# Attention over a cached K and V: the small load of x moves from the sync queue's second place to the head of ScalarE's queue

## The chip, the cores and the metric

The kernel runs on one core of a Trainium2 chip. The time is that of one execution on the device in microseconds. The kernel before takes 184.4 us, the median of three runs (184.36 to 184.57).

## The reference

A block of grouped-query attention for 8 sequences with 4 new tokens each. All arrays are bf16.

```
B, Sq, D = 8, 4, 512 ;  Hq, Hkv, Sk, Dh = 32, 8, 2048, 128 ;  rep = Hq // Hkv = 4
q = (x @ wq)                     # x [8,4,512], wq [512,4096] -> 32 heads of 128
s = q @ k_cache^T * Dh**-0.5     # k_cache [8,8,2048,128], each head of K serves 4 of q
p = softmax(s) ;  o = p @ v_cache
out = o @ wo                     # wo [4096,512] -> [8,4,512]
```

K and V are 33.6 MB each, wq and wo 4.2 MB each, x and the output 32 KB each. So nearly all of the 75.5 MB that are read are used once.

## The kernel before

**Staging.** K and V go through a ring of four slots in SBUF (`ring`, `NR = 4`), each of 4 MB, that is 32 KB in each of the 128 partitions. wq and wo pass through the same ring, a slot each. The list `loads` gives their order: K0 and x together ("k0"), wq, K1, V0, K2, V1, K3, and so on to V7, then wo. `issue(done)` (line 157) issues loads while fewer than four slots are taken. The call `issue(0)` at the start thus issues K0, x, wq, K1 and V0 at once; after each step of the main loop `issue(2 + 2 * u)` asks for what has come free, and each of those issues waits on its queue until the slot's last reader is done.

**Queues.** All loads are issued on the sync engine's queue, in order, but one: K0 comes in two halves (`by_member`), the first on the sync queue and the second on ScalarE's (`load_kv`, line 133, with the engines `(nc.sync, nc.scalar)`). x follows on the sync queue (line 163) and wq behind it (line 137). A queue hands out its transfers in order; the packets of both queues are carried by the same 16 DMA engines.

**Steps.** There are eight steps of K and V (`NU = 8`); each holds 16 heads of 2048 keys divided among partitions. For each step: VectorE turns K into 32x32 blocks (`turn`, line 213), TensorE forms the scores against a block-diagonal arrangement of the queries (`scores`, line 251), VectorE takes the maxima (`top`), ScalarE the exponentials (`exps`, line 291), VectorE turns the weights (line 305), ScalarE and GpSimd put them in block-diagonal form (line 315), TensorE multiplies them with V (`values`, line 331), and short operations scale and rearrange the result. The program order is written by hand (`manual_schedule`); the values of a step come after the scores of the next.

**The beginning,** where x is used: VectorE and GpSimd clear tiles; VectorE turns the first two quarters of K0 in four operations (line 413, the first and third read the first half of K0, the second and fourth the other one). TensorE transposes x against an identity (line 416), ScalarE copies the result to SBUF as `xT_sb` (line 419), TensorE multiplies with wq in 32 matmuls (line 425), ScalarE copies the queries out (line 432), VectorE transposes them (line 436), and GpSimd spreads them in the block-diagonal tile (`queries`, line 231). Then the scores of step 0 begin.

**The end:** wo's second half is loaded in four pieces (line 146), and `project` (line 403) multiplies by each as it lands. Two copies bring the result out of PSUM (lines 482 and 483), and one DMA stores it (line 484).

Of the kernel before, what the change touches and what calls it, by code (L numbers as in the profile page):

```python
# [17 lines left out]
def kernel(  # L18
# [9 lines left out]
    nc = tc.nc  # L28
# [45 lines left out]
    x_sb = const.tile([T, D], BF16, name="x_sb")  # L74
# [13 lines left out]
    def single(u):  # L88
        return FIRST < u < LAST

    def half_of(u):
        return NG - 1 if u == LAST else 0
# [8 lines left out]
    def take(key):  # L101
        slot_of[key] = n_loads[0] % NR
        n_loads[0] += 1
        return slot_of[key]
# [5 lines left out]
    def load_kv(kind, u, parts, engines=(nc.sync,)):  # L110

        slot = take((kind, u))
        cache = k_cache if kind == "k" else v_cache
        n = C * Dh
        if not single(u):
            rows = cache[NS1:, G * half_of(u) : G * half_of(u) + G].rearrange(
                "b g (s c) d -> (g s) b (c d)", c=C
            )
        elif kind == "v":
            rows = cache[u - 1].rearrange("(b g) (s c) d -> (g s) b (c d)", g=G, c=C)  # L120
        else:
            rows = cache[u - 1].rearrange("h (s c) d -> (h s) (c d)", c=NS * C)
        if kind == "k" and single(u):
            pairs = [(ring[:, slot, :, :].rearrange("p b n -> p (b n)"), rows)]
        elif parts is by_member:
            pairs = [(ring[:, slot, b, :], rows[:, b]) for b in range(NB)]
        else:
            pairs = [
                (ring[:, slot, :, int(h0 * n) : int(h1 * n)], rows[:, :, int(h0 * n) : int(h1 * n)])
                for h0, h1 in parts  # L130
            ]
        for i, (to, of) in enumerate(pairs):
            engines[i % len(engines)].dma_start(to, of)

    def load_wq():
        slot = take("wq")
        nc.sync.dma_start(
            ring[:, slot, :, :].rearrange("p b n -> p (b n)"), wq.rearrange("(p r) n -> p (r n)", r=R)
        )

    def load_wo():
        slot = take("wo")
        for gg, cuts in ((0, (0, RW)), (1, (0, 8, 13, 15, RW))):
            rows = wo[gg * G * 512 : (gg + 1) * G * 512, :].rearrange("(p r) j -> p (r j)", r=RW)
            for r0, r1 in zip(cuts, cuts[1:]):
                nc.sync.dma_start(ring[:, slot, gg, r0 * D : r1 * D], rows[:, r0 * D : r1 * D])
# [10 lines left out]
    def issue(done):  # L157

        while loads and n_loads[0] < done + NR:
            what = loads.pop()  # L160
            if what == "k0":
                load_kv("k", 0, by_member, (nc.sync, nc.scalar))
                nc.sync.dma_start(x_sb[:, :], x.flatten_outer_dims())
            elif what == "wq":
                load_wq()
            elif what == "wo":
                load_wo()
            elif what in split:
                load_kv(*what, by_member)
            else:  # L170
                load_kv(*what, by_half if what == ("v", NU - 1) else whole)

    issue(0)

    make_identity(nc, ident[:])
# [266 lines left out]
    for u in range(NU + 1):  # L442
# [19 lines left out]
        if u >= 1:  # L462
# [7 lines left out]
            if u == NU:  # L470
                joined(u - 1)
        issue(2 + 2 * u)

    o_last = psum_o.tile([128, DH], FP32, tag="o", name="o_last")
# [40 lines left out]
```

## Time and profile before

| what | value |
|---|---|
| median of three runs | 184.4 us (184.36 to 184.57) |
| time of the profiled execution | 184.38 us |
| its span, from the first to the last instruction | 182.5 us |
| TensorE / VectorE / ScalarE / GpSimd busy | 75% / 71% / 39% / 22% of the span |
| read from HBM | 75.53 MB, 414 GB/s over the span |
| x from issue to landing | 12.1 us |
| second half of K0 (ScalarE's queue) from issue to landing | 12.4 us |
| wq from issue to landing | 21.0 us |
| the store of the output, 32 KB, from issue to landing | 1.5 us |

The span is what the profile covers; 1.9 us of the execution lie outside it. The landing times hold all the waiting that a transfer does behind others, on its own queue and on the engines that both queues share, so they tell how much is queued ahead and not what a transfer costs. q1 in the profile is the sync queue, q10 is ScalarE's; q8 and q14 carry instructions. In the profile an engine's name with a q behind it (SPq, ACTq) is its sequencer, which issues DMAs, and ACT, DVE, POOL, PE and SP are ScalarE, VectorE, GpSimd, TensorE and the sync engine.

### The profile page before, as it was taken

How to read it: one execution, taken by the hardware profiler on the slowest of the kernel's cores; microseconds unless marked ns; L12 is line 12 of the kernel's file. 1: busy time of each engine (PE TensorE's matmuls, PEld its weight loads, DVE VectorE, ACT ScalarE, POOL GpSimd, SP SyncE). 2: the span in 40 equal slices, each digit the busy share in tenths (PEclk: the TensorE clock that was granted, in tenths of full speed). 3: DMA queues.
4: the chain of work that ended last, by engine and by line, in shares of the span. 5: the costliest groups of instructions: out<-in, count | busy, mean ns of one | idle time of the engine just before them, and what ended most of it. 6: DMA issues, size and time to landing. Idle time of an engine off the chain costs nothing.

```text
span 182.5 us, 2386 instructions
## 1 busy us (share of the span) xinstructions
PE 136.6 (75%) x924; PEld 83.3 (46%) x924; DVE 128.7 (71%) x161; ACT 70.3 (39%) x91; POOL 39.3 (22%) x110
## 2 busy tenths in 40 slices
PE   0000076940999999998999898989399977899993
PEld 0000022310348635843783485358234852388971
DVE  6518025738994999599689957995399559967340
ACT  2000020019604940990395079109900792063010
POOL 8800006006200700430080035004400220023000
PEclk9999999995589999999999999999969999999999
DMA  6999999999999998999999999999999999999991
GB/s 226 431 485 395 424 460 406 424 445 449 452 384 427 456 461 382 420 460 452 391 417 453 460 402 418 431 478 424 391 435 424 435 427 435 415 426 438 427 385 42
DMA packets 4938, 75.70 MB, mean 415 GB/s; under 512 B 512, under 2 KB 704, under 8 KB 960
## 3 DMA queue, kind: packets, MB, share of 16 engines
q1 hardware_dynamic: 4784, 73.47, 94.3%
q10 hardware_dynamic: 144, 2.10, 2.8%
q8 instruction: 7, 0.11, 0.2%
q14 instruction: 3, 0.02, 0.0%
HBM read 75.53 MB, written 0.03 MB: 414 GB/s over the span
## 4 chain that ended last, share of the span: by engine, by line
DMA 42%; DVE 23%; PE 22%; issue 4%; ACT 3%; POOL 2%; SPq 1%; ACTq 0%; DVEq 0%; POOLq 0%
DMA ring<-in_wo_dram 16%; PE s_ps L251 16%; DMA ring<-in_k_cache_dram 15%; DVE kt L213 14%; DMA ring<-in_wq_dram 12%; DVE stat L264 4%; PE o_ps L331 4%; ACT p_sb L291 3%; PE psq L425 2%; DVE pt L305 2%; DVE stat L322 1%; POOL p_bd L315 1%; POOL q_bd L231 1%; PE s_ps L403 1%; DVE stat L272 0%
## 5 line engine op out<-in xcount | busy, mean ns | idle before, releaser
L251 PE MATMUL s_ps<-kt,q_bd 128*128 128x512 bf16 x256 | 69.5, 409 | 20.0 <-POOL q_bd L231 9.9
L213 DVE STREAM_TRANSPOSE kt<-ring 128x1024 f32<-128x1024 f32 x64 | 73.9, 1210 | 14.2 <-DMA ring<-in_k_cache_dram 11.4
L331 PE MATMUL o_ps<-ring,p_bd 128*128 128x256 bf16 x512 | 57.2, 273 | 0.0
L251 PEld LDWEIGHTS <-q_bd 128*128 128x128 bf16 x256 | 25.3, 102 | 63.0 <-issue 26.6
L331 PEld LDWEIGHTS <-p_bd 128*128 128x128 bf16 x512 | 49.8, 98 | 6.0 <-issue 0.2
L315 ACT COPY p_bd<-pt 32x1024 bf16<-32x1024 bf16 x44 | 45.8, 1041 | 1.5 <-DVE pt L305 1.1
L291 ACT ACTIVATE p_sb<-s_ps,stat 128x1024 bf16<-128x1024 f32 x16 | 17.7, 1110 | 72.2 <-DVE stat L272 72.2
L315 POOL COPY p_bd<-pt 32x1024 bf16<-32x1024 bf16 x16 | 17.0, 1065 | 105.9 <-DVE pt L305 93.2
L264 DVE TENSOR_REDUCE stat<-s_ps 128x1 f32<-128x1024 f32 x16 | 19.3, 1208 | 3.4 <-PE s_ps L251 3.4
L305 DVE STREAM_TRANSPOSE pt<-p_sb 128x512 f32<-128x512 f32 x16 | 11.4, 712 | 14.0 <-ACT p_sb L291 14.0
L231 POOL COPY q_bd<-qT 32x64 bf16<-32x64 bf16 x64 | 13.1, 231 | 20.7 <-DVE qT L436 19.0
L425 PE MATMUL psq<-ring,xT_sb 128*32 128x512 bf16 x32 | 3.6, 630 | 9.1 <-DMA ring<-in_wq_dram 9.1
L416 PE MATMUL xtp<-ident,x_sb 32*128 32x32 bf16 x4 | 0.3, 195 | 13.3 <-DMA x_sb<-in_x_dram 13.3
L436 DVE STREAM_TRANSPOSE qT<-q_sb 128x64 f32<-128x64 f32 x8 | 1.2, 214 | 8.8 <-ACT q_sb L432 8.8
L177 DVE MEMSET p_bd<- 128x2048 uint32 x3 | 5.3, 1765 | 2.0 <-PEq L499 1.2
L322 DVE TENSOR_SCALAR stat<-of_b,stat 128x2 f32<-128x2 f32 x8 | 6.3, 793 | 0.3
L416 PEld LDWEIGHTS <-x_sb 32*128 32x128 bf16 x4 | 0.2, 117 | 13.3 <-DMA x_sb<-in_x_dram 13.3
L425 PEld LDWEIGHTS <-xT_sb 128*32 128x32 bf16 x32 | 1.3, 140 | 10.5 <-issue 10.1
L432 ACT CAST q_sb<-psq 128x512 bf16<-128x512 f32 x2 | 1.2, 586 | 11.8 <-PE psq L425 11.8
L375 PEld LDWEIGHTS <-perm 128*128 128x128 bf16 x56 | 3.8, 97 | 2.0 <-issue 0.5
L419 ACT COPY xT_sb<-xtp 128x128 bf16<-128x128 bf16 x1 | 0.3, 266 | 11.2 <-PE xtp L416 11.2
L343 ACT ACTIVATE o_sb<-o_ps,stat 128x128 bf16<-128x128 f32 x8 | 2.9, 368 | 4.1 <-PE o_ps L331 3.9
(30 smaller groups left out, 46.4 us busy)
## 6 DMA issues: line engine op xcount, KB each, us to landing
ring<-in_k_cache_dram SPq DMA_DIRECT2D x6, 4096.0 KB, 22.7
ring<-in_v_cache_dram SPq DMA_DIRECT2D x12, 2048.0 KB, 23.6
ring<-in_v_cache_dram SPq DMA_DIRECT2D x2, 4096.0 KB, 29.6
ring<-in_k_cache_dram SPq DMA_DIRECT2D x3, 2048.0 KB, 27.2
ring<-in_wq_dram SPq DMA_DIRECT2D x1, 4096.0 KB, 21.0
ring<-in_k_cache_dram ACTq DMA_DIRECT2D x1, 2048.0 KB, 12.4
ring<-in_wo_dram SPq DMA_DIRECT2D x1, 2048.0 KB, 25.9
ring<-in_wo_dram SPq DMA_DIRECT2D x1, 1024.0 KB, 28.2
```

The costliest lines, as they stand in the source:

```text
L177: nc.vector.memset(t[:, :, :, :, :], 0.0)
L213: nc.vector.transpose(out=out, in_=in_)
L231: nc.gpsimd.tensor_copy(out=qb[k * 32 : (k + 1) * 32, m, :, g, b, :].rearrange("w (j e) q -> w j e q", e=2), in_=qT[of * 32 : (of + 1) * 3 ...
L251: nc.tensor.matmul(s_ps[t // 2][:, t % 2, :], lhsT=q_bd[u % 2][:, m, 2 * j + e, :, :, :].rearrange("w g b q -> w (g b q)"), rhs=rhs, start ...
L264: nc.vector.tensor_reduce(out=stats[u][0][:, h : h + 1], in_=s_ps[h][:, :, :].rearrange("q t n -> q (t n)"), axis=AX, op=ALU.max, negate=True,
L291: nc.scalar.activation(out=out, in_=in_, func=EXP, bias=stats[u][1][:, :], scale=scale, accum_out=stats[u][2][:, h : h + 1],)
L305: nc.vector.transpose(out=pt[:, :, :, :].rearrange("s c q e -> s (c q e)").bitcast(FP32), in_=ps[u, h][:, :, :, :].rearrange("q c s e -> q ...
L315: copy(out=pb[rows, :, g, :, :], in_=pt[rows, :, :, :])
L322: nc.vector.tensor_scalar_mul(stats[u][3][:, :], of_b[:, :], stats[u][4][:, :])
L331: nc.tensor.matmul(o_pss[u][:, :, :], lhsT=pbs[u, h][:, i // 2, :, :, i % 2].rearrange("s g q -> s (g q)"), rhs=v[:, :, key_of(u, h, i // ...
L375: nc.tensor.matmul(o_pms[r // 2][:, r % 2, gg, :], lhsT=perm[:, r, w : w + 128], rhs=o_sbs[u][:, b, :], start=(u == 0 and r % 2 == 0 and g ...
L425: nc.tensor.matmul(psq[g * T : (g + 1) * T, :], lhsT=xT_sb[:, r, :], rhs=w[:, (g * NB + gg) * rep * Dh : (g * NB + gg + 1) * rep * Dh], st ...
```

## The change

x is no longer issued on the sync queue between the first half of K0 and wq. It is issued on ScalarE's queue, ahead of the second half of K0. So the sync queue holds the first half of K0, wq, K1 and V0 in this order, and ScalarE's queue x and then the second half of K0. Nothing else changes.

```
             if what == "k0":
+                nc.scalar.dma_start(x_sb[:, :], x.flatten_outer_dims())
                 load_kv("k", 0, by_member, (nc.sync, nc.scalar))
-                nc.sync.dma_start(x_sb[:, :], x.flatten_outer_dims())
```

## The prediction

> **What bounds the kernel now.** I read the DMA row and the queues of the page first, because the kernel moves 75.7 MB and computes little with it; then the windows, to see whether that row has a gap anywhere; then the chain that ended last and the start of the timeline.
>
> The page, part 2 (busy tenths in 40 slices of 4.56 us) and part 3 (packets, MB, share of 16 engines):
>
> ```profile
> DMA  6999999999999998999999999999999999999991
> DMA packets 4938, 75.70 MB, mean 415 GB/s; under 512 B 512, under 2 KB 704, under 8 KB 960
> q1 hardware_dynamic: 4784, 73.47, 94.3%
> q10 hardware_dynamic: 144, 2.10, 2.8%
> q8 instruction: 7, 0.11, 0.2%
> ```
>
> q1 is the sync queue's, q10 ScalarE's, whose only load is half of the first K. The shares sum to 97.3%; of a span of 182.5 us that is 177.6 us of packet time on each of the 16 engines. The packet records of the trace begin at 1.75 us, and the last piece of wo, issued at 151.39, lands 28.0 us later, at 179.4. Between the two lie 177.6 us. So from the first packet to the last landing there is no gap: the kernel's time is the start of the stream, its bytes, and a tail.
>
> The windows (busy time of each engine, then PEclk, DMA share, GB/s) say the same stage by stage:
>
> ```profile
> 2.00:30.00 28.00, 4.95 (x39) 1.98 (x40) 12.86 (x19) 1.89 (x4) 8.69 (x24) 1.00 1.00 425
> 30.00:60.00 30.00, 22.93 (x107) 11.09 (x105) 20.33 (x23) 11.38 (x15) 6.17 (x22) 0.83 1.00 429
> 60.00:90.00 30.00, 28.11 (x180) 16.36 (x178) 27.44 (x33) 15.10 (x19) 6.59 (x20) 1.00 1.01 434
> 120.00:150.00 30.00, 26.33 (x187) 17.68 (x186) 21.28 (x27) 16.15 (x20) 6.55 (x18) 0.94 1.00 429
> ```
>
> The last two figures are what to see: a share of 1.00 in every stage, even where the matmul clock was granted at 0.83.
>
> The chain that ended last, its pieces around the change and the one that decides the end (start, duration):
>
> ```profile
> 1.19 0.41 SPq L163
> ...
> 1.65 21.02 DMA ring<-in_wq_dram
> ...
> 22.72 3.63 PE psq L425 x31
> ...
> 149.32 29.10 DMA ring<-in_wo_dram
> ```
>
> The removed issue (L163) stands in this chain, just ahead of wq, so at first sight its 0.46 us looks like time to win. But a 4 MB load that needs 21.02 us to land is queued behind others: at the 429 GB/s of the windows its own 4.19 MB take 9.8 us. It is waiting for bytes, not for its issue.
>
> The start of the timeline, and what the early waits were for:
>
> ```profile
> 0.74 0.40 ACTq L133 DMA_DIRECT2D ring<-in_k_cache_dram  x1
> 0.75 0.38 SPq L133 DMA_DIRECT2D ring<-in_k_cache_dram  x1
> 1.17 1.28 ACT L419 ACT_TABLE_LOAD   x1 [1.17 <-PEq L499]
> 1.19 0.41 SPq L163 DMA_DIRECT2D x_sb<-in_x_dram  x1
> 1.65 0.41 SPq L137 DMA_DIRECT2D ring<-in_wq_dram  x1
> ```
>
> ```profile
> PE xtp L416 <- DMA x_sb<-in_x_dram: 13.3, 1, 13.3
> PE psq L425 <- DMA ring<-in_wq_dram: 9.1, 1, 9.1
> ```
>
> x arrives at 13.3 because it lies behind a half of K on the same queue. What it feeds is done at 14.0, and TensorE then waits another 9 us for wq: x has 8.7 us to spare.
>
> **The change, part by part.** The sum is made against the profiled execution: a span of 182.5 in a time of 184.38 us (1.9 outside the span); the median of the three runs is 184.4, so no correction is needed.
>
> *x leaves the sync queue.* One issue (0.41 and 0.05 to the next) goes. The wq, K1 and two V issues come 0.46 us earlier, the first at about 1.19. All of them then stand in a queue whose first load runs until about 12 us: worth 0. In the trace every later load up to the end of wo is issued at least 7 us before the load ahead of it has landed (the least is K2: issued at 35.01, V0 landing at 42.1), so nothing that moves by half a microsecond at the start can open a gap there.
>
> *x heads ScalarE's queue.* Its 32 rows of 1 KB are two packets on each engine, at a median of 0.046 us in the packet records, plus a semaphore write of 0.01: 0.10 us of each engine, moved from 12 us to the start of the same stream. Bytes and packets are unchanged: 0. x should land between 3 and 4 us rather than at 13.3 (q10's first packets begin at 2.45 to 3.24), and the ScalarE copy of its transpose (L419, now at 13.69) runs at about 4. Its table load slides behind one more issue, to about 1.6 to 2.9, still ahead of that copy. TensorE then waits for wq until 22.7 as before: 0.
>
> *The second half of K0 is issued 0.46 us later,* at 1.20 on ScalarE. The first half came on the engines 1.00 us after its issue (0.75 to 1.75), so this one is ready at about 2.2, before q10 had a turn on any engine at all (2.45). It ends perhaps 0.1 to 0.5 later, because the sync queue has a lead in the round between the two, and the engines then serve wq's packets in turn with it. Its reader is VectorE's second turn, which starts only at 14.2 behind the first one. All four turns end at 17.6, and VectorE then idles 7.7 us for the queries: 7 us of cover. Without that cover the price would be the 0.5.
>
> By the Trainium skill (DMA: Bandwidth & Descriptors, Anatomy of one DMA), a transfer costs about 2.0 us plus bytes over 436 GB/s, which makes x an estimated 2.1 us rather than 0.1. If the stream paid that at its head, the sum would be 186.5; the trace differs, since the windows leave no room for such a pause around x at 12 us, and the page itself lays most of the 2 us on the receipt and not on the moving of bytes.
>
> *The ramp* is the one thing that the trace doesn't show: what x's rows cost as first packets. Two DMA windows (packets, MB, share of 16 engines), 1.7 to 3.3 us and then 4 to 11.8:
>
> ```profile
> q1 hardware_dynamic: 17, 0.28, 60.5%
> q10 hardware_dynamic: 16, 0.26, 48.6%
> ...
> q10 hardware_dynamic: 109, 1.79, 53.4%
> q1 hardware_dynamic: 97, 1.59, 47.5%
> ```
>
> The share times 16 engines times the window, by the count: 0.91 us a packet on q1 and 0.78 on q10 at the start, 0.61 on both later. So an engine's first packets cost 0.30 and 0.17 us over the steady price. Upper bound: each of x's two rows pays 0.30 over its 0.05 and K's packet behind it is then cheap (-0.17): +0.43. Lower bound: x's rows ride along and neither first packet of K is slowed: -0.47. I take 0, near the middle; the three runs, each with a ramp of its own, differ by only 0.21 us in all.
>
> Sum: 184.38 + 0 + 0 + 0 = 184.4 us. No change.
>
> **The rivals.**
> *Slower by the ramp.* The two rows are paid dearly while all engines start at once. It decides once a row costs over 0.27 more than its steady price (2 x 0.27 - 0.17 = 0.37, which is 0.2%); at the bound the time is 184.8. For it: first packets are the dearest of the stream. Against: a row is a sixteenth of such a packet, and what makes it wait may be waited for only once.
> *Faster by the ramp.* ScalarE's queue starts with a tiny load, so the first packets of the sync queue do not compete with a second queue's: up to -0.47, 183.9. Against: q10's first packets already begin only after q1's.
> *Faster by the issue.* wq lands 0.46 earlier, and all behind it: 183.9. For it: L163 stands in the chain. Against: the 21 us to land, and 97.3% of DMA share.
> *The stream waits for x.* Both queues begin only when x has landed. The nearest row is the output's store, of the same 32 KB, 1.5 us from issue to landing; that would give 185.9. Against: the queues ran side by side from the first packets on. The skill's 2.1 us above is its sentence.
> *A fetch lands badly.* The seven q8 packets of 16 KB take 0.93 us each, on different engines as far as the final landings show (a group ends 0.9 later than the rest); two on one engine would add 0.93: 185.3. Nothing in the change touches them.
> *It does not do what it says* can hardly be: another queue is named in the code.
>
> **How the numbers follow.** About 0.2% of 184.4, 0.37 us, is what a measurement can tell from no change here. No change 0.80; slower by the ramp 0.07, by a wait for x 0.02, by a fetch 0.03: slower 0.12. Faster by the ramp 0.06, by the issue 0.02: faster 0.08. The range takes most of the ramp's bounds: 184.0 to 184.9, leaving out less than 0.2. The likeliest, 184.4, is the prediction.
>
> **What the profile after would show.** Right: x's issue first on ScalarE at 0.74 and K's at about 1.2, x landed before 4, TensorE's x transposes near 4 and an idle of some 18 us behind them, wq's first matmul again at 22.5 to 22.9, DMA shares of 1.00 in all windows, and the last wo landing at 179.4, give or take 0.3. Wrong: a first packet later than 1.75, a DMA share clearly under the 1.00 between 2 and 30 us, or a final landing that moves by more than 0.4.

## The result and the profile after

The changed kernel takes 185.0 us. Its ratio to the kernel before is 1.0031, with a 95% interval from 1.0019 to 1.0044: 0.35 to 0.8 us slower. Repeated on the chip that ran part of the experiments it was 1.0024 (1.0014 to 1.0034). The forecast was no change, 184.4 us in a range of 184.0 to 184.9. The profiled execution took 185.11 us, of which the span is 183.2; before it was 184.38 and 182.5.

(The kernel before lay between 184.4 and 184.7 us from one set of runs to the next, so times of different sets are compared by their ratios. Some profiles show an execution that was disturbed later on, and of those only the first 7 us are read.)

The DMA row and the queues, from parts 2 and 3 of the page after:

```profile
DMA  5999998999989999999899999999899999999991
...
DMA packets 4938, 75.70 MB, mean 413 GB/s; under 512 B 512, under 2 KB 704, under 8 KB 960
...
q1 hardware_dynamic: 4736, 73.44, 93.9%
q10 hardware_dynamic: 192, 2.13, 2.8%
q8 instruction: 7, 0.11, 0.2%
```

Packets and bytes are the same to the last one; 48 packets (x's 32 rows and 16 semaphore writes) have moved from q1 to q10. The first digit is 5 and was 6. Most of the loss lies there: 0.54 of the 0.73 us between the two profiled executions, as the packets below show.

The windows of the kernel after, between 2 and 90 us, do not show it: they are full again.

```profile
2.00:30.00 28.00, 4.50 (x39) 1.85 (x40) 12.66 (x19) 2.37 (x4) 8.27 (x22) 1.00 1.01 427
30.00:60.00 30.00, 22.76 (x128) 12.46 (x126) 23.07 (x29) 13.92 (x18) 8.89 (x30) 0.89 0.98 422
60.00:90.00 30.00, 28.27 (x180) 16.74 (x181) 26.23 (x30) 15.14 (x20) 5.05 (x14) 1.00 1.01 435
```

The start of the stream in slices of 0.75 us does (the last two figures are DMA share and GB/s). First the kernel before:

```profile
1.75:2.50 0.75, 0.00 (x0) 0.00 (x0) 0.75 (x1) 0.70 (x1) 0.75 (x2) 1.00 1.45 415
2.50:3.25 0.75, 0.00 (x0) 0.00 (x0) 0.51 (x1) 0.00 (x0) 0.75 (x2) 1.00 0.88 306
3.25:4.00 0.75, 0.00 (x0) 0.00 (x0) 0.62 (x1) 0.00 (x0) 0.75 (x1) 1.00 0.89 350
```

and the kernel after:

```profile
1.75:2.50 0.75, 0.00 (x0) 0.00 (x0) 0.75 (x1) 0.75 (x1) 0.75 (x2) 1.00 1.25 284
2.50:3.25 0.75, 0.00 (x0) 0.00 (x0) 0.51 (x1) 0.43 (x1) 0.75 (x2) 1.00 0.19 46
3.25:4.00 0.75, 0.00 (x0) 0.00 (x0) 0.62 (x1) 0.00 (x0) 0.75 (x1) 1.00 1.03 393
```

These views count a packet, with all its bytes and its whole duration, in the slice in which it starts: from 2.5 to 3.25 us 46 GB/s are started instead of 306. A low figure can thus mean that the engines are empty or that they still carry packets of the slice before (a share over 1.00). Here it is both. By the packet records an engine is occupied on the mean for 0.61 of the 0.75 us of this slice after, and for 0.74 before: many still carry a first packet of the sync queue, which lasts 1.10 us on the mean instead of 0.92. From 1.75 to 4 us an engine is occupied for 1.63 of 2.25 us, before for 2.09. The queues of that one slice, before and then after (packets, MB, share of 16 engines), tell who is missing:

```profile
q10 hardware_dynamic: 13, 0.21, 81.2%
q1 hardware_dynamic: 1, 0.02, 6.3%
```

```profile
q1 hardware_dynamic: 2, 0.03, 13.9%
q10 hardware_dynamic: 2, 0.00, 4.8%
```

The sync queue is as good as absent in both. Its first 16 packets, of 16 KB, begin from 1.75 us on, and its seventeenth only at 3.21 before and 3.32 after. The records do not name the engine of a packet, but there are 16 engines, so this is read as one packet per engine until then. Before, ScalarE's half of K0 fills that time, 13 packets of 16 KB in this slice. After, its queue starts two rows of 1 KB. They come late, too: x's first row begins at 3.05, where K's first packet began at 2.45, though both were issued at 0.74. Summed from the packet records, with a packet's bytes spread evenly over its duration, the stream after is 0.20 us of its steady rate behind at 2.5 us, 0.22 at 2.75, 0.54 at 4, and then 0.51 to 0.54 at the points looked at up to 177 us. It is neither caught up nor does it grow.

The chain that ended last, after, where it passes wq and wo:

```profile
1.17 21.96 DMA ring<-in_wq_dram
23.13 0.04 issue
23.17 3.63 PE psq L425 x24
...
149.82 29.29 DMA ring<-in_wo_dram
```

wq is issued 0.48 us earlier and arrives 0.45 later, and the last piece of wo, at 180.0, 0.7 later. The queues at the start and the early waits, after:

```profile
0.74 0.40 ACTq L162 DMA_DIRECT2D x_sb<-in_x_dram  x1
...
0.75 0.37 SPq L133 DMA_DIRECT2D ring<-in_k_cache_dram  x1
...
1.17 0.45 ACTq L133 DMA_DIRECT2D ring<-in_k_cache_dram  x1
1.17 0.42 SPq L137 DMA_DIRECT2D ring<-in_wq_dram  x1
```

```profile
PE psq L425 <- DMA ring<-in_wq_dram: 17.2, 1, 17.2
DVE kt L213 <- DMA ring<-in_k_cache_dram: 9.6, 2, 6.0
PE xtp L416 <- DMA x_sb<-in_x_dram: 5.6, 1, 5.6
```

x is there at 5.6 us instead of 13.3, and TensorE spends the gain waiting for wq: 17.2 us instead of 9.1.

### The profile page after: what moved, and what is told of

The parts are those of the page before. It is cut to its first block, busy times and chain, and to the rows that moved or that the text cites. A ratio compares the mean times of both kernels' runs of the same rounds, so it can differ in the third digit from the quotient of the medians.

```text
span 183.2 us, 2386 instructions
## 1 busy us (share of the span) xinstructions
PE 134.5 (73%) x924; PEld 82.9 (45%) x924; DVE 128.8 (70%) x161; ACT 70.2 (38%) x91; POOL 39.1 (21%) x110
## 4 chain that ended last, share of the span: by engine, by line
DMA 57%; DVE 17%; PE 16%; issue 3%; POOL 2%; ACT 2%; SPq 1%; ACTq 0%; POOLq 0%; DVEq 0%
DMA ring<-in_k_cache_dram 29%; DMA ring<-in_wo_dram 16%; DVE kt L213 13%; DMA ring<-in_wq_dram 12%; PE s_ps L251 10%; PE o_ps L331 4%; PE psq L425 2%; ACT p_sb L291 1%; DVE stat L264 1%; POOL p_bd L315 1%; DVE pt L305 1%; POOL q_bd L231 1%; PE s_ps L403 1%; DVE stat L322 0%; SPq L146 0%
## 5 line engine op out<-in xcount | busy, mean ns | idle before, releaser
L251 PE MATMUL s_ps<-kt,q_bd 128*128 128x512 bf16 x256 | 67.2, 402 | 22.1 <-DVE kt L213 10.0
L425 PE MATMUL psq<-ring,xT_sb 128*32 128x512 bf16 x32 | 3.6, 630 | 17.2 <-DMA ring<-in_wq_dram 17.2
L425 PEld LDWEIGHTS <-xT_sb 128*32 128x32 bf16 x32 | 1.3, 139 | 18.7 <-issue 18.3
L403 PE MATMUL s_ps<-ring,oP 128*32 128x256 bf16 x32 | 4.3, 272 | 0.6 <-DMA ring<-in_wo_dram 0.5
L403 PE MATMUL o_last<-ring,oP 128*32 128x256 bf16 x32 | 4.4, 274 | 0.0
## 6 DMA issues: line engine op xcount, KB each, us to landing
ring<-in_k_cache_dram SPq DMA_DIRECT2D x6, 4096.0 KB, 25.7
```

What stands on the lines that cost most here:

```text
L251: nc.tensor.matmul(s_ps[t // 2][:, t % 2, :], lhsT=q_bd[u % 2][:, m, 2 * j + e, :, :, :].rearrange("w g b q -> w (g b q)"), rhs=rhs, start ...
L403: nc.tensor.matmul(out_ps[half], lhsT=oP[gg][:, r, :], rhs=w[:, r, half * DH : (half + 1) * DH], start=(gg == 0 and r == 0), stop=(gg == N ...
L425: nc.tensor.matmul(psq[g * T : (g + 1) * T, :], lhsT=xT_sb[:, r, :], rhs=w[:, (g * NB + gg) * rep * Dh : (g * NB + gg + 1) * rep * Dh], st ...
```

## The experiments

Three theories were set against each other. Cover: what is lost is the bulk load (one of many large packets) at the head of the second queue, which fills the engines until the first queue's second packets come. Rows: the small rows of x are dear as first packets. Crowd: more transfers are issued in the first 1.6 us (wq among them), and that slows the first packets. Beside each time stands how far the stream is behind that of the kernel before at 5 us, by the packet records of one profile for each kernel. Diffs are against the kernel before.

### The change again

```
+                nc.scalar.dma_start(x_sb[:, :], x.flatten_outer_dims())
                 load_kv("k", 0, by_member, (nc.sync, nc.scalar))
-                nc.sync.dma_start(x_sb[:, :], x.flatten_outer_dims())
```

> The changed kernel once more, on the chip of the next three, so that they can be set beside it. Every theory: slower than before by 0.5 to 0.65 us; 46 GB/s or thereabouts between 2.5 and 3.25 us, where before has 306.

Ratio 1.0024 (1.0014 to 1.0034), 0.55 us behind at 5 us. From 2.5 to 3.25 us:

```profile
2.50:3.25 0.75, 0.00 (x0) 0.00 (x0) 0.51 (x1) 0.45 (x1) 0.75 (x2) 1.00 0.17 48
```

The hole in the starts is the change's own and not an accident of one execution: 48 GB/s where it was 46, and x's first row begins at 3.05 us again.

### K first, x behind it, both on ScalarE's queue

```
                 load_kv("k", 0, by_member, (nc.sync, nc.scalar))
-                nc.sync.dma_start(x_sb[:, :], x.flatten_outer_dims())
+                nc.scalar.dma_start(x_sb[:, :], x.flatten_outer_dims())
```

> ScalarE's queue holds the second half of K0 first and x behind it; the sync queue is as in the changed kernel (first half of K0, wq, K1). Cover theory: in the first 1.5 us a queue has only one packet per engine ready, and the 16 KB packets of ScalarE's half of K0 fill the engines until the sync queue's second packets come; with K at the head again the time is that of before, 184.4 us, and the stream is not behind at 30 us. Rows theory: the 1 KB rows of x are dear only as first packets; here they come behind a packet of K: 184.4 to 184.6. Crowd theory: x, both halves of K0 and wq are all issued within the first 1.6 us, wq 0.46 earlier than before, and that slows the first packets: 185.0, as the changed kernel.

Ratio 1.0000 (0.999 to 1.001), 0.07 us behind at 5 us.

```profile
2.50:3.25 0.75, 0.00 (x0) 0.00 (x0) 0.51 (x1) 0.45 (x1) 0.75 (x2) 1.00 0.86 284
```

It differs from the changed kernel only in the order of two issues on one queue, and the loss is gone. wq is issued as early as there (1.19 us), so the crowd of early issues is not the cause. That x leaves the sync queue is by itself worth nothing in either direction.

### x twice ahead of K

```
+                nc.scalar.dma_start(x_sb[:, :], x.flatten_outer_dims())
+                nc.scalar.dma_start(out_sb[:, :], x.flatten_outer_dims())
                 load_kv("k", 0, by_member, (nc.sync, nc.scalar))
-                nc.sync.dma_start(x_sb[:, :], x.flatten_outer_dims())
```

> ScalarE's queue holds x, a second load of x into the tile of the output (overwritten at the end), and then the second half of K0. Cover theory: after the sync queue's second packets have come nothing is missing, so the second copy adds only its bytes: 185.0 to 185.2 us. Rows theory: the price of the rows doubles: 185.5 to 185.7. Crowd theory: one more issue in the first microseconds, 185.2 to 185.4.

Ratio 1.0028 (1.0017 to 1.0039), 0.62 us behind at 5 us against the change's 0.54. Twice the rows cost 0.08 us more, which is about their bytes and packets and no more than two profiles of the same stretch can differ by (K late, next); the rows theory wanted half a microsecond. The rows themselves say the same: in the changed kernel the first 16 of them last 0.12 us on the mean (0.19 in its repeat), against 0.05 in the stream.

### K late, no small rows at all

```
+    hold = const.tile([1, 64], BF16, name="hold")
+    nc.vector.memset(p_bd[1][:, :, :, :, :], 0.0)
+    nc.scalar.copy(out=hold[:, :], in_=p_bd[1][:1, 0, 0, :, :].rearrange("p q e -> p (q e)"))
     issue(0)
...
-    for t in p_bd[1:]:
+    for t in p_bd[2:]:
```

> x stays in its old place on the sync queue; ScalarE's half of K0 is issued only once ScalarE has read a tile that VectorE clears first, so at about 3.1 us instead of 0.74, and its packets come at about 4.1. Cover theory: the missing second queue costs the same as in the changed kernel with no small row in sight: 184.9 to 185.1, 0.5 us behind at 30 us. Rows theory: 184.4. Crowd theory: 184.4 or less.

Ratio 1.0023 (1.0013 to 1.0033), 0.46 us behind at 5 us. The issue of K's half at 3.05 us instead of 0.74, and the slice:

```profile
3.05 0.38 ACTq L133 DMA_DIRECT2D ring<-in_k_cache_dram  x1
```

```profile
2.50:3.25 0.75, 0.00 (x0) 0.00 (x0) 0.51 (x1) 0.21 (x1) 0.75 (x2) 1.00 0.64 197
```

x is in its old place, and nearly the whole loss is there. With this the rows theory falls: it is K's absence that costs, and x's rows only keep K away. K's packets came even later than expected, at 6.75 us instead of 4.1. Up to then this kernel and the next one have the same packets on the same single queue, and yet they are 0.46 and 0.37 us behind: so losses of single profiles are good to about 0.1 us.

### One queue

```
-                load_kv("k", 0, by_member, (nc.sync, nc.scalar))
+                load_kv("k", 0, by_member)
```

> All loads on the sync queue (both halves of K0, x, wq, ...), none on ScalarE's. Cover theory: nothing fills the engines between the first and the second packet of the only queue: 184.9 to 185.1 us, the stream some 0.5 us behind at 30 us. Rows theory: x's rows lie far behind the first packets: 184.4. Crowd theory: fewer issues compete at the start: 184.4 or a little less.

Ratio 1.0021 (1.0010 to 1.0031), 0.37 us behind at 5 us.

```profile
1.75:2.50 0.75, 0.00 (x0) 0.00 (x0) 0.75 (x1) 0.27 (x1) 0.75 (x2) 1.00 1.79 350
2.50:3.25 0.75, 0.00 (x0) 0.00 (x0) 0.51 (x1) 0.00 (x0) 0.75 (x2) 1.00 0.29 87
```

The time is as the cover theory forecast, but not for its reason. The engines are not empty here: the packets that start before 2.5 us fill the next slice as well (share 1.79), and an engine is occupied for 2.03 us of the 2.25 from 1.75 to 4, against 2.09 before. It is the first packets that last longer, 1.21 us on the mean against 0.92. Why they do is open.

The second queue for K0, which looks like a mere saving of an issue, is worth 0.2% to the kernel before. The Trainium skill (DMA: Bandwidth & Descriptors, "Issuing engines are not separate DMA queues") says that starting transfers from several engines saves only the sequencer's time. In the steady stream the windows agree with it, with a share of 1.00 on the sync queue alone. At the start that is doubtful here: the second half of K0 is issued 0.4 us later than before, about what is lost, but the first half had packets left for every engine by then, and with quarters on one queue (below) an issue that is as late goes with a loss of 0.24 us. No run separates the two.

### x at the head of the sync queue

```
+                nc.sync.dma_start(x_sb[:, :], x.flatten_outer_dims())
                 load_kv("k", 0, by_member, (nc.sync, nc.scalar))
-                nc.sync.dma_start(x_sb[:, :], x.flatten_outer_dims())
```

> x heads the sync queue instead (x, first half of K0, wq); ScalarE's queue has the second half of K0 alone, issued at 0.74. Cover theory: the two queues are alike, so it costs the same whichever of them starts with the small rows: slower than before by 0.4 to 0.6 us, the same hole between 2.5 and 3.25 us. If the loss hung on ScalarE's queue or on K0's second half coming late, it would be 0 here, since that half is at the head of its queue again.

Ratio 1.0040 (1.0026 to 1.0053), 0.57 us behind at 5 us. By the start of the stream it does not matter which queue starts with the rows; the time, 0.74 us slower, lies above the forecast of 0.4 to 0.6, though its interval (0.5 to 1.0) reaches into it. The hole comes earlier here, since the rows are now the first thing on the engines:

```profile
1.75:2.50 0.75, 0.00 (x0) 0.00 (x0) 0.75 (x1) 0.71 (x1) 0.75 (x2) 1.00 0.77 59
2.50:3.25 0.75, 0.00 (x0) 0.00 (x0) 0.51 (x1) 0.00 (x0) 0.75 (x2) 1.00 0.77 240
```

This run doesn't tell cover from rows. As the first thing on the engines the rows are dear: the first 16 last 0.57 us on the mean, against 0.05 in the stream, and that alone is about the loss. In the changed kernel, where they come behind the sync queue's packets, they are not.

### K0 in quarters, on two queues and on one

```
             pairs = [(ring[:, slot, b, :], rows[:, b]) for b in range(NB)]
+            if u == 0 and kind == "k":
+                pairs = [
+                    (ring[:, slot, b, h * n // 2 : (h + 1) * n // 2], rows[:, b, h * n // 2 : (h + 1) * n // 2])
+                    for h in range(2)
+                    for b in range(NB)
+                ]
```

On two queues:

> K0 in four quarters, alternately on the sync and on ScalarE's queue, so that the first packets of both queues are of 8 KB and not of 16; x on the sync queue behind them. Cover theory, if what counts is the bytes of each queue's first packet on an engine: 32 engine-packets of 8 KB fill 0.3 us each and leave a hole until about 3.25: slower than before by 0.2 to 0.5 us. If what counts is only that a transfer of many rows is at the head of each queue: within 0.1 us of before.

Ratio 1.0003 (0.9991 to 1.0014), 0.03 us behind at 5 us. So the bytes of the first packets are not what counts: the cover theory by bytes was wrong, the plain one holds. With packets of 8 KB the second ones of a queue begin at 2.8 us instead of 3.2, and the engines stay filled.

With the same quarters, all on the sync queue (as in the one-queue kernel):

> All of K0 on the sync queue, as with one queue before, but in quarters, so that the first packets are of 8 KB. Settles what cover needs. If it is a second queue with bulk at its head: slower than before by 0.3 to 0.45 us, the same as one queue with packets of 16 KB. If it is only that enough packets can be in hand on an engine at once, of whatever queue: within 0.15 us of before.

Ratio 1.0032 (1.0018 to 1.0046), 0.6 us slower and so above both forecasts; behind at 5 us by 0.24 us, where one queue with packets of 16 KB was 0.37. The time speaks for the need of a second queue; by the start of the stream smaller packets take over a third of its work. The difference in time to the two-queue version, 0.3%, is larger than the 0.2 us that the start explains, and that rest stays open.

### GpSimd's queue as the cover

```
-                load_kv("k", 0, by_member, (nc.sync, nc.scalar))
-                nc.sync.dma_start(x_sb[:, :], x.flatten_outer_dims())
+                nc.scalar.dma_start(x_sb[:, :], x.flatten_outer_dims())
+                load_kv("k", 0, by_member, (nc.sync, nc.gpsimd))
```

> x alone on ScalarE's queue, the first half of K0 on the sync queue, the second half on GpSimd's. The rows of x head a queue as in the changed kernel, but the second half of K0 no longer stands behind them. Cover theory: the hole between 2.5 and 3.25 us is as small as GpSimd's packets come early; if they come by 2.5 us, within 0.15 us of before, if only after 3.3 us, slower by 0.4 to 0.6 as the changed kernel. Rows theory: slower by 0.5 either way.

Ratio 1.0033 (1.0019 to 1.0047), 0.56 us behind at 5 us. GpSimd issues at 1.25 us, but in the packet records its first packet begins at 5.89, so it covers nothing. x's first row begins at 3.35.

```profile
2.50:3.25 0.75, 0.00 (x0) 0.00 (x0) 0.51 (x1) 0.00 (x0) 0.75 (x1) 1.00 0.05 22
```

### Three queues

```
         slot = take("wq")
-        nc.sync.dma_start(
+        nc.gpsimd.dma_start(
```

> The kernel before, but wq on GpSimd's queue, so that three queues with bulk loads start together. Cover theory with more cover: the stretch from 2.5 to 4 us moves more than before and the time falls by up to 0.3 us; if GpSimd's packets come after 3.3 us, no change. K0 then lands some 7 us later, near wq, and the scores of step 0 start about 1 us later, inside the 7 us of cover.

Ratio 1.0006 (0.9993 to 1.002): no gain. GpSimd's packets of wq come as late as in the last experiment. In this kernel's one profile the stream is 0.29 us behind at 5 us: the sync queue's first packets last 1.32 us on the mean, and ScalarE's begin at 3.03 instead of 2.45. This execution took 184.97 us, three others 184.54 to 184.60. So the start differs from one execution to the next, and a bulk load at the head of both queues does not always prevent a loss.

### wq first

```
-                load_kv("k", 0, by_member, (nc.sync, nc.scalar))
-                nc.sync.dma_start(x_sb[:, :], x.flatten_outer_dims())
+                load_kv("k", 0, by_member, (nc.scalar,))
             elif what == "wq":
                 load_wq()
+                nc.sync.dma_start(x_sb[:, :], x.flatten_outer_dims())
```

> The sync queue starts with wq, whose packets are of 32 KB, and then x; ScalarE's queue has both halves of K0. Cover theory by bytes: the first packets hold 48 KB per engine instead of 32, so the stretch from 1.75 to 4 us moves as much as before or more: from 0.3 us faster to the same. The scores of step 0 begin some microseconds later, which the 7 us that the stream is ahead of the loads cover. If late queries or late K0 counted at the end after all, it would be slower by 1 us or more.

Ratio 1.018 (1.013 to 1.024), far off the expectation. The stream is 0.31 us behind at 5 us, but most of the loss comes later. The sync queue's wait before K2's issue, and the window in which it tells:

```profile
SPq L133 <- DMA ring<-in_k_cache_dram: 27.2, 1, 27.2
```

```profile
30.00:60.00 30.00, 16.62 (x58) 6.39 (x58) 23.17 (x32) 8.43 (x10) 7.69 (x32) 0.72 0.93 392
```

Here an engine takes one packet from each queue in turn, as the packet records show. Against wq's packets of 32 KB, K0's of 16 KB get a third of the engines, and the second half of K0 lands at 30.4 us instead of 13.1. VectorE is done with K0's slot so late that K2 is issued at 42.35, when V0 lands at 42.56: of the 7 us of cover 0.2 are left. That is too little, as K2's first packet starts 0.96 us after its issue, at 43.31, and for over a microsecond no packet starts:

```profile
42.20:43.30 1.10, 1.10 (x6) 0.48 (x5) 1.10 (x2) 0.00 (x0) 0.00 (x0) 1.00 0.00 0
```

The stream, 0.32 us behind at 40 us, is 2.75 behind at 60. Here compute does reach the end, which it does not in the change itself.

## Why the prediction was wrong

**What bounds the kernel** was right, and the experiments rest on it: the stream is without a gap after 4 us, and 0.54 us that are lost at its start are still missing at 177 us and in the time.

**The step that failed is the ramp.** It was called the one thing that the trace doesn't show, bounded by -0.47 and +0.43, and put at 0 "near the middle". It measured +0.53 us. The upper bound was built on the wrong mechanism, x's two rows each paying a first packet's surcharge of 0.30 us; the first of the two paid 0.07 (0.15 in the repeat). Twice the rows cost 0.08 us more, and K0 late without any rows costs nearly the same. What was not asked is what ScalarE's packets were doing between 2.45 and 3.2 us. The two rows shown for the start held it: 17 packets of q1 and 16 of q10 up to 3.3 us, so one per engine from each queue. The sync queue's first packets, 0.92 us each on the mean, do not fill the time from 1.75 to 3.2, and with K away from the head of the other queue nothing large comes beside them. The bound that follows from those rows is 16 packets at 0.61 us, 0.6 us per engine, close to what was lost. How the loss comes about is mixed: an engine is empty for 0.46 us more than before in this profile and for 0.35 in its repeat (1.75 to 4 us), and the rest goes with the sync queue's first packets, which last 1.10 and 1.17 us. Why a queue's second packets, and x's first row, come so late stays open.

**K0's second half issued 0.46 us later** was put at 0 because its packets would be ready at 2.2 us, before q10 had a turn at all, and would end 0.1 to 0.5 later. Turns counted for more. x's first row came at 3.05, its two rows and a semaphore write each took a turn of q10 against a 16 KB packet of q1, and one more turn went to q1, for a reason that the records do not show; so K's first packet on q10 began at 5.80 us. And once the sync queue had come to wq's packets of 32 KB, K's of 16 KB had the smaller part. It landed at 18.3 us, 5.2 later. The Trainium skill (DMA: Bandwidth & Descriptors, Queues, rings and completion order) has the engines go round the queues packet by packet, and this trace agrees: 67 packets of q1 and 64 of q10 between 11.1 and 18 us. That delay itself did cost nothing, as the cover of 7 us was there: the last of VectorE's four early turns ended at 21.8, ahead of its transposes of the queries at 25.7.

**x leaves the sync queue: 0.** Right: with K first and x behind it, the same early wq gives the time of before.

**x early: 0.** Right in value. x landed at 5.6 and not between 3 and 4, and its copy ran at 6.0; both wait for wq as forecast.

**The rivals.** "Slower by the ramp", at 0.07, had the place and the sign, with the rows as its price. "Faster by the issue" is refuted by K first and x behind it, where wq is issued as early and nothing is won, and "faster by the ramp" by the measured time. A stream that waits for x is not what happened: the first packets begin at 1.75 as before. Nor is it a fetch: the first 16 KB packet of q8 begins at 51.5 us, when the loss is long complete. The 2.1 us that the prediction worked out by the Trainium skill (DMA: Bandwidth & Descriptors, Anatomy of one DMA) rest on a fit that the page gives for transfers issued by GpSimd, and x is issued by ScalarE; no such pause is in the stream. The signs that were named for a wrong forecast, a DMA share clearly under 1.00 between 2 and 30 us, could not have shown it, since a loss of half a microsecond is 2% of such a window; the last wo landing, 0.7 later, did.

**The size.** 184.38 and 0.53 make 184.9, the upper end of the range. The profiled execution has 185.1: wo's last piece lands on the 16 engines over 2.0 us there (178.0 to 180.0), over 1.8 before (177.5 to 179.4), and the output waits for the last of them. The repeat of the change lands the same, 178.0 to 180.0, and K first with x behind it from 177.8 to 179.5. That would fit engines that do not all lose the same at the start, which was not followed engine by engine.

## What to carry to other kernels

In a kernel that is bound by its DMA stream, look at the first two microseconds of the stream in slices, not in windows of a stage: time lost there was not made up in any of these runs. Head both the sync and ScalarE's queue with a bulk load, and put a small one behind it, unless someone waits for it at once; here that is worth 0.2 to 0.4%. And where two queues share the engines, count turns, not bytes: a small packet takes a turn as a large one does, so a load behind it comes later, and a load of half the other queue's packet size gets a third of the engines.

## What the runs showed of the hardware

The sync queue's first packets of 16 KB begin 1.0 us after the start of their issue (0.75 to 1.75), ScalarE's 1.7 before (0.74 to 2.45) and 2.3 with three queues (0.74 to 3.03). x's first row at the head of ScalarE's queue begins 2.3 us after its issue in the change and 2.6 beside GpSimd's queue (0.75 to 3.35). GpSimd's first packets begin 4.6 to 4.9 us after the start of its issue (1.25 to 5.89 and to 6.15).

The sync queue's first packets last 0.92 us on the mean before and 0.99 with K first and x behind it, 1.10 to 1.27 in kernels without a bulk load at the head of the second queue and 1.32 in the profile with three queues, against 0.61 in the steady stream. Its seventeenth packet, the first that must be some engine's second, begins at 2.46 us with one queue (2.95 with K late), at 3.21 before and at 3.32 after. Why it comes so late was not settled; with packets of 8 KB it begins at 2.34 us with one queue and at 2.78 with two.
